# One relu per gate chunk on VectorE, weight scaling one step later, two PSUM copies on ScalarE, and a joined step in block 19 of a fused attention and gated-MLP kernel

## The chip, the cores and the metric

The kernel runs on one core of a Trainium2 chip. The core has five engines that the texts below name: TensorE (PE for matmuls, PEld for the loads of their weights), VectorE (DVE), ScalarE (ACT), GpSimd (POOL) and SyncE (SP), which issues the transfers. Each engine works through its own instruction list in order and waits on semaphores for the others. The metric is the device time of one execution in microseconds (us), and the comparison is between medians of several runs.

## The reference

A layer norm of `x` (2048 tokens, 512 features) feeds an attention over a cache (32 heads, 2048 cached keys, head size 128) and a gated MLP of width 1792 whose gate goes through a relu. Their product is added to `x`.

```python
xn = _layernorm(x)
# attention
q = (xn @ wq)                                   # 2048 x 4096, split into 32 heads
scores = einsum("bhqd,bhkd->bhqk", q, k_cache) * (128 ** -0.5)
p = softmax(scores)
s = einsum("bhqk,bhkd->bhqd", p, v_cache) @ wo
# gated MLP
gate = xn @ W_gate
up = xn @ W_up
gate = gate * (gate > 0)
g = silu((gate * up) @ W_down)
out = x + s * g
```

## The kernel before

**Attention as the main loop.** The work is cut into 128 blocks. Block `b` is one head and one quarter of the queries (512 of them), so four blocks make a head. A block has 8 pairs, numbered `p` 0 to 7; a pair is 256 keys. For a pair TensorE makes two score matmuls of 512 columns (`emit_S_tile`, L1441), ScalarE takes the exponential of both at once (L1453, 128x1024, from PSUM into `PT`), and three pairs later TensorE makes eight matmuls of 129 columns with `V_sb` (`emit_PV_tile`, L1550). `gp` counts the pairs whose scores are made, `gq = gp - 3` those whose values are. After a block VectorE divides by the row sums (L1470, L1473).

**The side work.** All the other products are set between the pairs: the query projections, the MLP's gate and up products for two of the four quarters, its down product, and the output projection. They are done in a seven-product form: a 2 by 2 product of blocks is made from seven smaller products, numbered 1 to 7, and the sums of them that VectorE adds up from PSUM. A few of the matrices' blocks are summed beforehand, on GpSimd or VectorE. So one projection is made in steps, each with one or two products:

- `emit_st(pr, c, step)` projects the queries of heads `2*pr` and `2*pr+1`, for the quarters `c` and `c+2`, in four steps (products 1 and 2; 6 and 5; 7 and 3; 4). The running sums lie in `cu` and `cv`, the results go to `QT_sb` (L871 to L928).
- `emit_gu` makes one product of one of 14 chunks of the gate and up products. In the order 1, 2, 6, 5, 7, 3, 4 it gives the gate of one quarter (`gA`, after product 2), the up of the other quarter (`uB`, product 7), its gate (`gB`, product 3) and the first quarter's up (`uA`, product 4). The relu and the product of gate and up are `gu_h` on GpSimd (L1101, L1103). Two such products share one place in the plan, so that product 1 of a chunk falls now on the first, now on the second of the two; in the second case its copy out of PSUM is on ScalarE (L1136), in the first on VectorE (L1139).
- The weights of a chunk are loaded three chunks ahead into `W2`; `gu_sums` scales them on ScalarE (L608) and sums their blocks on GpSimd (L613 to L618). It is called when `gu_later` says so: eight products after the load.
- `emit_d(Q, step)` is the down product of a quarter in four steps, with a tanh on ScalarE (L1201) and a multiplication on VectorE (L1206) one and two pairs later; `emit_hs` makes the sums it needs on VectorE (L780 to L789).
- `emit_os` is the output projection of a group of four heads, `emit_unit` a query projection of 28 smaller products for the later groups.

**What orders it.** `plan` says which items are issued at which pair `(b, p)` of the values, `side` which helpers; `qp3` is a table of places for the projection of the fourth pair of heads in the blocks 18 to 20. In the main loop the scores of pair `gp` come first, then the items, then the helpers, then the values of pair `gq`. If a block's first item has one product (`early`), the scores of the next pair are issued ahead of it.

**The ring.** The scores and the products share three PSUM slots of two banks each. A pair of scores takes one slot, released by its exponential. `emit_M` takes one slot for its list of items, released when the last of VectorE's additions out of it is done:

```python
        def emit_M(items):
            s = ring_acquire()          # waits for what released the slot last
            for fn, nb, *args in items:
                t = fn(*args, *range(k, k + nb))
                toks += t if isinstance(t, list) else [t]
            ring_tok[s] = toks
```

The slots are handed out in turn, so in a stretch with one pair and one `emit_M` at each place an `emit_M` needs the exponential of the pair before, and the next scores need the additions of the `emit_M` before.

## Time and profile before

| | |
|---|---|
| median of 3 runs | 1245.6 us (1245.51 to 1245.78) |
| profiled execution | 1245.94 us, of which its span 1244.6 us |
| PE busy in the span | 1225.7 us (98%) |
| ACT busy | 1031.3 us (83%) |
| DVE busy | 854.5 us (69%) |
| POOL busy | 715.2 us (57%) |
| granted TensorE clock | 1.00 in every stretch asked for |

A timeline row of the profile gives the start in us from the span's start, the duration in us, the engine, the source line, the operation, the tiles written and read, and how many like instructions the row merges; in square brackets stands the engine's idle time before the row, with what ended it. Matmuls are pipelined: the record of one lasts longer than the time after which the next can start, so TensorE loses time also where the records show little idle time. Lost time is read from the starts: a row's start, plus the number of its matmuls times their spacing, is when the next row could have begun.

### The profile page before, as it was taken

The numbers are of one execution on the slowest core, as the hardware profiler recorded it, in microseconds if no ns is written. First come the engines' busy times: TensorE is split into PE (matmuls) and PEld (weight loads), VectorE is DVE, ScalarE is ACT, GpSimd is POOL, SyncE is SP. The second block draws the span as 40 slices with busy tenths as digits, with TensorE's granted clock in tenths as the row PEclk, the third lists the DMA queues.
The fourth block names the chain that finished last, engine by engine and source line by source line (L and its number), as shares of the span: only waits on it lengthen the run. The fifth ranks groups of instructions, "written<-read, shape, count | busy, mean of one in ns | idle before, by whom it ended". The sixth has DMA issues, their size and how long they took to land.

```text
span 1244.6 us, 30670 instructions
## 1 busy us (share of the span) xinstructions
PE 1225.7 (98%) x12413; PEld 890.3 (72%) x12647; DVE 854.5 (69%) x1652; ACT 1031.3 (83%) x1107; POOL 715.2 (57%) x944
## 2 busy tenths in 40 slices
PE   9999999999999999999999999999999999999998
PEld 5466565776777777777777777777777777777775
DVE  6677776666666767676666667667666676666667
ACT  3457777668888988988988989989989989889994
POOL 3383999514656578547864687557862786550002
PEclk9999999999999999999999999999999999999999
DMA  9712331221322332232222332332222223444312
GB/s 275 157 31 35 73 77 31 52 43 28 56 52 52 65 69 52 48 70 51 47 38 48 77 61 48 52 70 65 53 52 49 51 53 48 52 68 74 77 36 76
DMA packets 250699, 78.14 MB, mean 63 GB/s; under 512 B 226240, under 2 KB 250560, under 8 KB 250560
## 3 DMA queue, kind: packets, MB, share of 16 engines
q1 hardware_dynamic: 249888, 75.79, 31.5%
q8 instruction: 100, 1.64, 0.6%
q10 hardware_dynamic: 672, 0.39, 0.1%
q14 instruction: 39, 0.32, 0.1%
HBM read 38.54 MB, written 2.10 MB: 33 GB/s over the span
## 4 chain that ended last, share of the span: by engine, by line
PE 85%; issue 8%; ACT 3%; POOL 2%; DVE 2%; DMA 0%; POOLq 0%; DVEq 0%
PE ps_acc L1550 33%; PE ps_r L1441 29%; PE ps_r L1322 6%; PE ps_r L1023 6%; PE ps_r L1125 3%; ACT PT L1453 3%; PE ps_r L1184 2%; PE ps_r L706 2%; PE ps_r L710 2%; PE ps_r L891 2%; PE ps_acc L809 1%; DVE UVR L1028 1%; POOL g_sb L1605 0%; POOL hT L1103 0%; POOL gB L1101 0%
## 5 line engine op out<-in xcount | busy, mean ns | idle before, releaser
L1453 ACT ACTIVATE PT<-ps_r 128x1024 bf16<-128x1024 f32 x1024 | 980.8, 1030 | 142.6 <-PE ps_r L1441 130.8
L1550 PE MATMUL ps_acc<-V_sb,PT 128*128 128x129 bf16 x8192 | 687.8, 220 | 5.3
L1550 PEld LDWEIGHTS ps_acc<-V_sb,PT 128*128 128x128 bf16 x8192 | 574.8, 98 | 144.7 <-ACT PT L1453 2.4
L1441 PE MATMUL ps_r<-QT_sb,KT_sb 128*128 128x512 bf16 x1823 | 600.6, 379 | 5.6 <-DVE QT_sb L896 0.5
L1028 DVE TENSOR_TENSOR UVR<-UVR,ps_r 128x256 f32<-128x256 f32 (+1 forms) x456 | 198.2, 454 | 160.9 <-PE ps_r L1023 156.2
L1340 DVE TENSOR_TENSOR s_acc<-s_acc,ps_r 128x512 f32<-128x512 f32 x264 | 167.7, 683 | 15.8 <-PE ps_r L1322 15.8
L1441 PEld LDWEIGHTS ps_r<-QT_sb,KT_sb 128*128 128x128 bf16 x2048 | 171.6, 98 | 8.4 <-DVE QT_sb L896 1.0
L998 POOL TENSOR_TENSOR TI<-xn_sb 128x256 f16<-128x256 f16 x96 | 66.8, 695 | 88.9 <-PE ps_r L1023 88.1
L1473 DVE TENSOR_TENSOR Onorm<-ps_acc,rz_sb 128x512 bf16<-128x512 f32 x127 | 87.8, 691 | 4.4
L1091 POOL TENSOR_TENSOR UVR<-UVR,UVR 128x1024 f32<-128x1024 f32 x12 | 28.3, 2362 | 98.8 <-DVE UVR L1028 98.8
L1028 DVE TENSOR_TENSOR QT_sb<-UVR,ps_r 128x256 bf16<-128x256 f32 x144 | 57.5, 419 | 27.8 <-PE ps_r L1023 22.8
L1605 POOL TENSOR_TENSOR g_sb<-s_acc,WX 128x512 bf16<-128x512 f32 x6 | 6.8, 1155 | 108.0 <-DVE WX L1598 108.0
L1023 PE MATMUL ps_r<-TI,SI 128*128 128x256 f16 x252 | 68.7, 273 | 0.0
L998 POOL TENSOR_TENSOR TI<-xn_sb,TI 128x256 f16<-128x256 f16 x96 | 67.8, 706 | 0.0
L998 POOL TENSOR_TENSOR TI<-xnT 128x256 f16<-128x256 bf16 x72 | 50.6, 703 | 27.2 <-PE ps_r L1023 27.2
L1470 DVE RECIPROCAL rz_sb<-ps_acc 128x4 f32<-128x4 f32 x127 | 23.2, 182 | 62.3 <-PE ps_acc L1550 59.5
L972 POOL TENSOR_SCALAR Wq_sb<-Wq_sb 128x1024 bf16<-128x1024 bf16 x12 | 33.2, 2770 | 49.8 <-DMA Wq_sb<-in_A_wq_dram 49.8
L1097 POOL TENSOR_TENSOR QT_sb<-UVR,UVR 128x512 bf16<-128x512 f32 x24 | 30.0, 1273 | 38.1 <-DVE UVR L1028 38.1
L1027 DVE COPY UVR<-ps_r 128x256 f32<-128x256 f32 x72 | 28.1, 419 | 33.6 <-PE ps_r L1023 33.6
L998 POOL TENSOR_TENSOR TI<-xnT,TI 128x256 f16<-128x256 bf16 x72 | 50.6, 703 | 0.0
L998 POOL TENSOR_TENSOR SI<-SO 128x128 f16<-128x128 f16 x96 | 49.2, 513 | 0.0
L1023 PEld LDWEIGHTS ps_r<-TI,SI 128*128 128x128 f16 x252 | 24.3, 97 | 34.1 <-DVE QT_sb L1028 6.7
(184 smaller groups left out, 1355.2 us busy)
## 6 DMA issues: line engine op xcount, KB each, us to landing
V_sb<-in_A_v_cache_dram SPq DMA_DIRECT2D x32, 512.0 KB, 4.6
Wq_sb<-in_A_wq_dram SPq DMA_DIRECT2D x16, 256.0 KB, 3.2
Wo_sb<-in_A_wo_dram SPq DMA_DIRECT2D x8, 512.0 KB, 4.6
xr_sb<-in_A_x_dram SPq DMA_DIRECT2D x16, 128.0 KB, 2.1
OT_store<-Onorm SPq DMA_TRANSPOSE x127, 2.5
Wd_sb<-in_B_W_down_dram SPq DMA_DIRECT2D x1, 1792.0 KB, 14.4
W<-in_B_W_gate_dram SPq DMA_DIRECT2D x14, 128.0 KB, 2.4
W<-in_B_W_up_dram SPq DMA_DIRECT2D x14, 128.0 KB, 3.1
```

The source lines that it names most:

```text
L972: wu_tok[(g, i)] = sem_uo.sig(pool.tensor_scalar(w, w, WSC, None, op0=ALU.mult))
L998: return sem_ui.sig(pool.tensor_tensor(dst, x, y, o))
L1023: return sem_up.sig(pe.matmul(dst, lhs, rhs, start=start, stop=stop, skip_group_check=True))
L1028: dve.tensor_tensor(dst, x, ps, ALU.add))
L1097: pool.tensor_tensor(dst, UU[:, 2 * e:2 * e + 2, :], RR[:, 2 * e:2 * e + 2, :], ALU.add))
L1125: ins = pe.matmul(ps_r[:, bank, :], L(i), R(i), start=(i == 0), stop=(i == HC - 1))
L1322: ins = pe.matmul(ps_r[:, bank, j * DH:(j + 1) * DH], L(i), R(i), start=(i == 0 and j == 0), stop=(i == GH - 1 and j == 1))
L1340: t = dve.tensor_tensor(names[k], names[k], view(bank), op)
L1441: ins = pe.matmul(ps_r[:, 2 * s + tt, :], KT_sb[h % 2][:, t * 128:(t + 1) * 128], QT_sb[qt_slot[(h, Q)]][:], start=True, stop=True)
L1453: act.activation(PT[pb][:], ps_r[:, 2 * s:2 * s + 2, :], ACTF.Exp, scale=scale / WSC)
L1473: dve.tensor_tensor(Onorm[ob][:], o_ap, rz_sb[:].to_broadcast([128, 4, Dh]), ALU.mult))
L1550: ins = pe.matmul(o_ap, PT[pb][:, tt, j * 128:(j + 1) * 128], V_sb[vb][:, t, 0:VW], start=(t == 0 and j % 2 == 0), stop=(t == KT - 1 and j ...
```

## The change

Five edits, all in the first 20 of the 128 blocks:

1. The relu of `gA` moves from GpSimd to VectorE, right behind the addition that makes `gA` (the relu of `gB` stays).
2. `gu_sums` (the scaling on ScalarE and the sums on GpSimd) is called nine products after the load, no longer eight.
3. Two copies out of PSUM move from VectorE to ScalarE: product 1 of the second half of the first projection (`cu`), and product 1 of the down product of quarter 2 (`c_u`).
4. In step 2 of every four-step projection product 3 is made before product 7, and the addition that uses it (`QT_sb` of the first head) stands ahead of the one into `cu`. In block 0 the last of the helpers `emit_hs` of quarter 2 moves from pair 4 to pair 6.
5. In the blocks 18 and 19 the projection's steps move to one or two pairs earlier; step 3 is joined with the output projection's step at the start of block 19, in one slot.

```diff
@@ emit_st @@
                 p1 = prod(1, banks[0])
                 p2 = prod(2, banks[1])
-                _wait(dve, p1)
-                st_tok["u"] = sem_qpe.sig(dve.tensor_copy(cu[:], ps_r[:, banks[0], :]))
+                if pr == 0 and c == 1:
+                    _wait_all(act, [p1, st_tok["r"]])
+                    st_tok["u"] = sem_qpa.sig(act.copy(cu[:], ps_r[:, banks[0], :]))
+                else:
+                    _wait(dve, p1)
+                    st_tok["u"] = sem_qpe.sig(dve.tensor_copy(cu[:], ps_r[:, banks[0], :]))
                 r = qt_ready[(h0, Q0)] = comb(qt_take(h0, Q0), cu[:], banks[1], waits=(p2, st_tok["u"]))
...
             if step == 2:
+                p3 = prod(3, banks[1])
                 p7 = prod(7, banks[0])
-                p3 = prod(3, banks[1])
+                qt_ready[(h0, Q1)] = comb(qt_take(h0, Q1), cv[:], banks[1], waits=(p3, st_tok["v"]))
                 st_tok["u"] = comb(cu[:], cu[:], banks[0], waits=(p7, st_tok["u"]))
-                r = qt_ready[(h1, Q1)] = comb(qt_take(h1, Q1), cv[:], banks[0], waits=(st_tok["v"],))
-                r = qt_ready[(h0, Q1)] = comb(qt_take(h0, Q1), cv[:], banks[1], waits=(p3,))
+                r = qt_ready[(h1, Q1)] = comb(qt_take(h1, Q1), cv[:], banks[0])
                 return [r]
...
-        qp3 = {18: ((2, 0), (4, 1), (6, 2)), 19: ((2, 3), (4, 4), (6, 5)), 20: ((3, 6), (5, 7))}
+        qp3 = {18: ((1, 0), (3, 1), (5, 2)), 19: ((0, 3), (2, 4), (4, 5)), 20: ((3, 6), (5, 7))}
@@ gu_h, emit_gu @@
-            _wait(pool, sem_hp.sig(pool.tensor_scalar(gate, gate, 0.0, None, op0=ALU.max)))
+            if Q == 3:
+                _wait(pool, sem_hp.sig(pool.tensor_scalar(gate, gate, 0.0, None, op0=ALU.max)))
...
                 r = gu_tok["g1"] = comb(gA[k % 2][:], u[:], waits=(gu_tok["u"], h_done.get((1, k - 2))))
+                _wait(dve, r)
+                gu_tok["gr"] = sem_gud.sig(dve.tensor_scalar(gA[k % 2][:], gA[k % 2][:], 0.0, None, op0=ALU.max))
...
-                gu_h(1, k, gA[k % 2][:], uA[k % 2][:], [r, gu_tok["g1"]])
+                gu_h(1, k, gA[k % 2][:], uA[k % 2][:], [r, gu_tok.pop("gr")])
                 if k + NW < FC:
                     gu_load(k + NW)
-                    gu_later.append((gu_pos[0] + 8, k + NW))
+                    gu_later.append((gu_pos[0] + 9, k + NW))
@@ emit_d, step 0 @@
-                _wait(dve, p1)
-                d_tok["u"] = sem_dd.sig(dve.tensor_copy(c_u[:], view(banks[0])))
+                if Q == 2:
+                    _wait(act, p1)
+                    d_tok["u"] = sem_da.sig(act.copy(c_u[:], view(banks[0])))
+                else:
+                    _wait(dve, p1)
+                    d_tok["u"] = sem_dd.sig(dve.tensor_copy(c_u[:], view(banks[0])))
@@ the plan @@
-        hs_at = {2: [(1, k, 0, 1 + k) for k in range(4)]}
+        hs_at = {2: [(1, 0, 0, 1), (1, 1, 0, 2), (1, 2, 0, 3), (1, 3, 0, 6)]}
...
                     for p, step in qp3[b]:
-                        at(b, p, (emit_st, 1 if step % 4 == 3 else 2, 3, step // 4, step % 4))
+                        q = (emit_st, 1 if step % 4 == 3 else 2, 3, step // 4, step % 4)
+                        if p:
+                            at(b, p, q)
+                        else:
+                            at(b, p, o, q)
+                            o = None
```

VectorE in block 0, from the first down addition to the block's division. `dbuf_104` is `c_u`, `dbuf_106` the first output half, `HS_sb` and `hT` the down product's sums, `cuv_86` and `cuv_87` are `cu` and `cv`. Before:

```order
L789 TENSOR_TENSOR HS_sb_58<-hT_53,HS_sb_58 128x1024
L1218 COPY dbuf_104<-ps_r 128x512
L1193 TENSOR_TENSOR dbuf_106<-dbuf_104,ps_r 128x512
L780 TENSOR_TENSOR HS_sb_58<-hT_53 128x768
L783 TENSOR_TENSOR hT_53<-hT_53 128x3x256
L896 TENSOR_TENSOR cuv_86<-cuv_86,ps_r 128x512
L896 TENSOR_TENSOR cuv_87<-cuv_86,ps_r 128x512
L786 TENSOR_TENSOR HS_sb_58<-hT_53 128x768
L1206 TENSOR_SCALAR g_sb<-dbuf_108,dbuf_106 128x2x256
L789 TENSOR_TENSOR HS_sb_58<-hT_53,HS_sb_58 128x768
L896 TENSOR_TENSOR cuv_86<-cuv_86,ps_r 128x512
L896 TENSOR_TENSOR QT_sb<-cuv_87,ps_r 128x512 x2
```

And with the change, over the same stretch:

```order
L791 TENSOR_TENSOR HS_sb_58<-hT_53,HS_sb_58 128x1024
L1203 TENSOR_TENSOR dbuf_106<-dbuf_104,ps_r 128x512
L782 TENSOR_TENSOR HS_sb_58<-hT_53 128x768
L785 TENSOR_TENSOR hT_53<-hT_53 128x3x256
L898 TENSOR_TENSOR cuv_86<-cuv_86,ps_r 128x512
L898 TENSOR_TENSOR cuv_87<-cuv_86,ps_r 128x512
L788 TENSOR_TENSOR HS_sb_58<-hT_53 128x768
L1216 TENSOR_SCALAR g_sb<-dbuf_108,dbuf_106 128x2x256
L898 TENSOR_TENSOR QT_sb<-cuv_87,ps_r 128x512
L898 TENSOR_TENSOR cuv_86<-cuv_86,ps_r 128x512
L898 TENSOR_TENSOR QT_sb<-cuv_87,ps_r 128x512
L791 TENSOR_TENSOR HS_sb_58<-hT_53,HS_sb_58 128x768
```

The copy into `c_u` has left VectorE, and the last `HS_sb` sum stands behind the three additions of the projection's step 2.

ScalarE in the gate and up stretch, where the copy of product 1 is its own (`gcu`); `W_72` is a chunk's weights, `PT` the exponentials. Before:

```order
L1453 ACTIVATE PT<-ps_r 128x1024 x6
L1136 COPY gcu_95<-ps_r 128x512
L608 ACTIVATE W_72_89<-W_72_89 128x1024
L1453 ACTIVATE PT<-ps_r 128x1024 x2
L634 ACTIVATE Wq_sb<-Wq_sb 128x1024
```

With the change:

```order
L1467 ACTIVATE PT<-ps_r 128x1024 x6
L1144 COPY gcu_95<-ps_r 128x512
L1467 ACTIVATE PT<-ps_r 128x1024
L610 ACTIVATE W_72_89<-W_72_89 128x1024
L1467 ACTIVATE PT<-ps_r 128x1024
L636 ACTIVATE Wq_sb<-Wq_sb 128x1024
```

One exponential now stands between the copy and the scaling of the weights.

TensorE at the start of block 19: `WX` with `OT_store` is the output projection's one product, `Wq_sb` with `xn_sb` the query projection's product 4. Before:

```order
L1441 MATMUL ps_r<-QT_sb,KT_sb 128x512 x4
L1322 MATMUL ps_r<-WX_119,OT_store_76 128x256 x4
L1550 MATMUL ps_acc<-V_sb,PT 128x129 x16
L1441 MATMUL ps_r<-QT_sb,KT_sb 128x512 x2
L891 MATMUL ps_r<-xn_sb,Wq_sb 128x512 x2
L1550 MATMUL ps_acc<-V_sb,PT 128x129 x8
```

With the change:

```order
L1455 MATMUL ps_r<-QT_sb,KT_sb 128x512 x2
L1336 MATMUL ps_r<-WX_119,OT_store_76 128x256 x4
L893 MATMUL ps_r<-xn_sb,Wq_sb 128x512 x2
L1564 MATMUL ps_acc<-V_sb,PT 128x129 x8
L1455 MATMUL ps_r<-QT_sb,KT_sb 128x512
```

Both products now share one slot, and the scores of the next pair are no longer issued ahead of them.

More of the change, by code (lines that the diff above doesn't have):

```diff
@@ L266, in bass_recurrent_scan__mha_block_cached__glu_gated_reglu__prompt_kernel @@
         sem_qpe = newsem()
+        sem_qpa = newsem()
+        sem_da = newsem()
         sem_rz = newsem()
@@ L927, in emit_st @@
             r = qt_ready[(h1, Q0)] = comb(qt_take(h1, Q0), cu[:], banks[0], waits=(p4, st_tok["u"]))
+            st_tok["r"] = r
             return [r]
-        qp3 = {18: ((2, 0), (4, 1), (6, 2)), 19: ((2, 3), (4, 4), (6, 5)), 20: ((3, 6), (5, 7))}
+        qp3 = {18: ((1, 0), (3, 1), (5, 2)), 19: ((0, 3), (2, 4), (4, 5)), 20: ((3, 6), (5, 7))}
         unit_order = (1, 2, 6, 5, 3, 7, 4)
```

## The prediction

> **What bounds the kernel now.** I read the page first: which engine is full?
>
> ```profile
> PE 1225.7 (98%) x12413; PEld 890.3 (72%) x12647; DVE 854.5 (69%) x1652; ACT 1031.3 (83%) x1107; POOL 715.2 (57%) x944
> ```
>
> TensorE is. The five edits lie in blocks 0 to 19, so the second view is the busy time of that stretch (columns: window, its length, then busy time and instructions of PE, PEld, DVE, ACT, POOL).
>
> ```profile
> 66.00:311.00 245.00, 241.74 (x2167) 162.40 (x2205) 172.87 (x274) 178.60 (x194) 153.35 (x139) 1.00 0.25 47
> ```
>
> TensorE is idle for 245.0 - 241.7 = 3.3 us there, and the change neither removes a matmul nor narrows one. So about 3.3 us, 0.26% of the time, is all there is to gain, and a result under 1242.3 us would contradict the profile. The third view is the timeline: where do these 3.3 us lie, and who is late there? A matmul of 512 columns starts every 0.22 us and one of 129 every 0.057 us (rows below: x4 takes 1.03 where x2 takes 0.59, and x16 takes 1.07 where x4 takes 0.39).
>
> Block 0 has the two largest gaps:
>
> ```profile
> 78.78 0.59 PE L1441 MATMUL ps_r<-QT_sb,KT_sb 128*128 128x512 bf16 x2
> 79.66 0.39 PE L891 MATMUL ps_r<-xn_sb,SW 128*128 128x512 f16 x1 [0.28 <-DVE dbuf L1193]
> ```
>
> ```profile
> 85.59 0.39 PE L1550 MATMUL ps_acc<-V_sb,PT 128*128 128x129 bf16 x4
> 86.51 0.61 PE L1441 MATMUL ps_r<-QT_sb,KT_sb 128*128 128x512 bf16 x2 [0.54 <-DVE QT_sb L896]
> ```
>
> The first could start at 78.78 + 2 x 0.216 = 79.21 and starts 0.45 late; the second at 85.59 + 4 x 0.057 = 85.82, and starts 0.69 late. Both wait for VectorE to empty a PSUM slot. Between them TensorE loses another 0.4 us in small pieces to ScalarE, which runs without a pause there:
>
> ```profile
> 73.27 2.85 ACT L1453 ACTIVATE PT<-ps_r 128x1024 bf16<-128x1024 f32 x3 [0.27 <-PE ps_r L1441]
> 79.63 0.63 ACT L1201 ACTIVATE dbuf<-dbuf 128x512 f32<-128x512 f32 x1 [3.51 <-DVE dbuf L1193]
> ```
>
> ```profile
> 82.92 3.89 ACT L1453 ACTIVATE PT<-ps_r 128x1024 bf16<-128x1024 f32 x4
> ```
>
> Its tanh waited 3.51 us for the same VectorE addition, with two exponentials queued behind it.
>
> In the gate and up stretch GpSimd's sums are late once, and ScalarE's exponential five times:
>
> ```profile
> 145.59 0.59 PE L1441 MATMUL ps_r<-QT_sb,KT_sb 128*128 128x512 bf16 x2
> 146.41 0.81 PE L1125 MATMUL ps_r<-xn_sb,SG 128*128 128x512 f16 x3 [0.22 <-POOL SG L618]
> ```
>
> ```profile
> 172.38 0.59 PE L1441 MATMUL ps_r<-QT_sb,KT_sb 128*128 128x512 bf16 x2
> 172.94 0.39 PE L1125 MATMUL ps_r<-xn_sb,SG 128*128 128x512 f16 x1
> ```
>
> ```profile
> PEld ps_r L1125 <- ACT PT L1453: 2.2, 5, 0.5
> ```
>
> The first is 146.41 - 146.02 = 0.39 us, the second 172.94 - 172.81 = 0.13 us. The waits row (total, times, longest; window 128 to 200 us) has five like the second; a load normally idles some 0.1 us between matmuls and a wait takes more than that, so I count 0.14 us for four of them and 0.20 for the fifth with its neighbour: 0.76 us. At block 19 there is one more:
>
> ```profile
> 304.42 1.03 PE L1441 MATMUL ps_r<-QT_sb,KT_sb 128*128 128x512 bf16 x4
> 305.47 0.61 PE L1322 MATMUL ps_r<-WX,OT_store 128*128 128x256 f16 x4
> 305.92 1.07 PE L1550 MATMUL ps_acc<-V_sb,PT 128*128 128x129 bf16 x16
> ```
>
> 305.47 - 305.28 = 0.19 us. The sum is 0.45 + 0.69 + 0.4 + 0.39 + 0.76 + 0.19 = 2.9 us; the rest of the 3.3 is in places that no edit touches.
>
> **The change part by part.** *Copies on ScalarE and the order in block 0.*
>
> ```profile
> 72.40 0.69 DVE L905 COPY cuv<-ps_r 128x512 f32<-128x512 f32 x1 [0.18 <-PE ps_r L891]
> 73.20 0.69 DVE L896 TENSOR_TENSOR QT_sb<-cuv,ps_r 128x512 bf16<-128x512 f32 x1
> ```
>
> ```profile
> 78.13 0.68 DVE L1218 COPY dbuf<-ps_r 128x512 f32<-128x512 f32 x1
> 78.91 0.69 DVE L1193 TENSOR_TENSOR dbuf<-dbuf,ps_r 128x512 f32<-128x512 f32 x1
> ```
>
> ```profile
> 71.97 1.02 ACT L1453 ACTIVATE PT<-ps_r 128x1024 bf16<-128x1024 f32 x1 [0.70 <-PE ps_r L1441]
> ```
>
> ```profile
> 129.50 0.58 ACT L1136 COPY gcu<-ps_r 128x512 f32<-128x512 f32 x1
> 129.96 1.07 ACT L608 ACTIVATE W<-W 128x1024 bf16<-128x1024 bf16 x1
> ```
>
> ```profile
> 73.95 0.59 PE L1441 MATMUL ps_r<-QT_sb,KT_sb 128*128 128x512 bf16 x2
> ```
>
> The first copy costs, though it leaves VectorE. On ScalarE it stands behind the exponential that ends at 72.99, takes 0.58 (as the one at 129.50 does) and ends near 73.5; VectorE had its own copy done at 73.09. The addition into `QT_sb` so ends at 74.3, not 73.89. Queued behind it are VectorE's sums `HS_sb` (+0.4), and its slot goes to the scores of the fifth pair, which TensorE starts at 73.95: +0.37 us. The second copy is free: ScalarE is idle from 76.12 to 79.63, and the product is there at 76.5. VectorE saves its 0.78 (78.13 to 78.91) but comes 0.4 later, so the down addition ends at 79.3 and not 79.60. TensorE, 0.37 late, arrives at 79.6 and no longer waits: the 0.45 is nearly all paid back at the other place. ScalarE's tanh and the exponentials behind it come 0.3 earlier, and TensorE, which follows them to 85, with them. Then step 2:
>
> ```profile
> 82.57 1.15 DVE L1206 SCALAR_TENSOR_TENSOR g_sb<-dbuf,dbuf 128x512 bf16<-128x512 f32 x1
> 83.64 1.02 DVE L789 TENSOR_TENSOR HS_sb<-hT,HS_sb 128x768 f16<-128x768 f16 x1
> 84.58 0.68 DVE L896 TENSOR_TENSOR cuv<-cuv,ps_r 128x512 f32<-128x512 f32 x1
> 85.18 1.27 DVE L896 TENSOR_TENSOR QT_sb<-cuv,ps_r 128x512 bf16<-128x512 f32 x2
> ```
>
> Without L789 ahead of them the three additions (1.95 us) end at 83.4 + 1.95 = 85.35. TensorE arrives at 85.82 - 0.3 = 85.5: the 0.69 goes, by a margin of 0.1 us. L789 then runs to 86.3 and delays the block's division, whose banks TensorE wants again only 28 matmuls later. Sum of block 0: 0.69 + 0.3 = 1.0 us (bounds: 0.5 if the margin fails and the first copy is later, 1.5 if that copy delays nobody).
>
> *Relu on VectorE.* GpSimd loses 14 instructions of 1.49 us:
>
> ```profile
> L1101 POOL TENSOR_SCALAR gA<-gA 128x512 bf16<-128x512 bf16 x14 | 20.8, 1486 | 0.0
> ```
>
> ```profile
> L436 DVE TENSOR_SCALAR xc_sb<-x_sb,mv 128x512 bf16<-128x512 bf16 x4 | 1.4, 354 | 0.1
> ```
>
> Its sums come earlier by more than the 0.39 us they were late: 0.39 gained. VectorE gains 14 instructions. The nearest row is L436, 0.354 us for the same shape with a per-partition operand; L745 below does 7 times as many elements in 1.25 us, 0.18 for this size. I take 0.25. What is queued behind it are the additions of products 6, 5 and 7, whose slots TensorE waits for. Where the relu comes late in a pair of products (7 of 14 chunks) VectorE's play is smallest:
>
> ```profile
> 173.58 0.69 DVE L1131 TENSOR_TENSOR gcv<-gcu,ps_r 128x512 f32<-128x512 f32 x1 [0.38 <-PE ps_r L1125]
> ```
>
> ```profile
> 174.98 0.68 DVE L1131 TENSOR_TENSOR uB<-gcv,ps_r 128x512 bf16<-128x512 f32 x1
> ```
>
> ```profile
> 176.04 0.59 PE L1441 MATMUL ps_r<-QT_sb,KT_sb 128*128 128x512 bf16 x2
> ```
>
> 0.38 idle before `gcv`, and 0.38 from the end of `uB` to the matmul that takes its slot, less 0.1 for the signal and 0.14 for the earlier TensorE: 0.5 us of play. 0.25 us fits. But VectorE and GpSimd hold each other up:
>
> ```profile
> 53.27 0.67 POOL L644 TENSOR_TENSOR SW<-Wq_sb 128x256 f16<-128x256 bf16 x1 [18.34 <-DVE xn_sb L589]
> 53.90 1.52 POOL L645 TENSOR_TENSOR SW<-Wq_sb 128x256 f16<-128x256 bf16 x1
> ```
>
> ```profile
> 53.64 1.25 DVE L745 TENSOR_SCALAR Wd_sb<-Wd_sb 128x3584 bf16<-128x3584 bf16 x1
> ```
>
> GpSimd's second sum takes 1.52 where the first takes 0.67: it lasts until VectorE's L745 is over, plus its own 0.67. The same kind of instruction is now added 14 times beside a busy GpSimd. Where it stands in one of the late chunks:
>
> ```profile
> 171.85 1.16 POOL L1103 TENSOR_TENSOR hT<-gB,uB 128x512 f16<-128x512 bf16 x1
> ```
>
> ```profile
> 171.69 0.69 DVE L1131 TENSOR_TENSOR gA<-gcu,ps_r 128x512 bf16<-128x512 f32 x1 [1.02 <-PE ps_r L1125]
> ```
>
> `gA` is there at 172.38, the relu wants to start at 172.5, and this product of GpSimd lasts to 173.0; with a relu less ahead of it GpSimd is about 0.2 us further, so 0.3 are waited for, and 0.3 + 0.25 is 0.05 to 0.1 more than the play. In other late chunks GpSimd is by then waiting for the scaled weights and is free. I put 0.2 us for all of them.
>
> The Trainium skill (page SBUF — State Buffer, section "Who interferes with whom") calls this an exclusive lock: a VectorE tensor_scalar in a two-port mode and a GpSimd instruction do not share, the second waits for the whole of the first. The rows of L645 agree. By that rule alone, with no look at who is where, up to a whole GpSimd instruction would be waited for, which is the second rival below.
>
> *Scaling one step later.* Where the copy is ScalarE's, copy (0.58) and scaling (1.07) stood ahead of an exponential; now the scaling stands behind it. The exponential comes 1 us earlier, so the five waits (0.76) go. The next one ends where it did, and its slot is wanted 1.75 us (four products and a pair) later: no new wait, except 0.05 us where three exponentials now go ahead. GpSimd's sums start when the scaling is done, 1.1 later, but GpSimd was the later of the two. Gain 0.7.
>
> *Block 19.*
>
> ```profile
> 304.86 0.69 DVE L1473 TENSOR_TENSOR Onorm<-ps_acc,rz_sb 128x512 bf16<-128x512 f32 x1
> ```
>
> The joined slot needs the exponential of one pair further back, so the 0.19 goes. It is released after three additions (0.64 each, as in step 2's 1.27 for two) that follow this division, which ends at 305.55: at 307.5. TensorE has the joined products (0.87) from 304.86 on, then a pair's values and scores (0.89), the next values (0.45) and scores (0.43), and wants the slot at 307.5 less 0.1 for the signal: 0.1 lost. Gain 0.1; bounds -0.2 and 0.19.
>
> The sum: 1.0 + 0.39 - 0.2 + 0.7 + 0.1 = 2.0 us. The profiled execution is 1245.94 us, 1.34 more than its span of 1244.6; the median is 0.34 less than it. 1244.6 - 2.0 + 1.34 - 0.34 = 1243.6 us.
>
> **The rivals.** *All of it comes through* (0.27). The first copy delays nobody, the relu always fits: 1.5 + 0.39 + 0.76 + 0.19 = 2.8, so 1242.8 us. For it: ScalarE's copy may start earlier than I think, 0.1 inside the exponential's end. Against it: the fifth pair's scores wait for this one slot and had nothing to spare.
>
> *The relu is held up by GpSimd each time* (0.10). In each of the 7 late chunks it waits out a relu of `gB` of 1.49 us: 1.49 + 0.25 - 0.5 = 1.2 us, 8.7 in all, so 1252.3 us. From 0.65 us a chunk (4.5 in all) the kernel is slower by more than 0.2%. Against it: after the change GpSimd is idle for part of each chunk, and in three of the seven it waits for the scaling at that time.
>
> *The waits only move* (0.20). The delayed exponentials and the later copy give back what was won, and only the 0.69 and 0.39 are kept: 1244.5 us. For it: ScalarE has the same work in the same stretch, and a copy more.
>
> **How the numbers follow.** My forecast has 0.43. About 0.2%, 2.5 us, is what a measurement tells from no change. Only the first rival (0.27) and a tenth of my own case lie below 1243.1: faster 0.30. The rest of it and the moved waits: same 0.60. Slower 0.10. The range takes in the full gain and a bad half of the relu's waits: 1242.5 to 1245.9; my own case alone has 1242.9 to 1244.4.
>
> **What would show it.** Right: the matmuls at 79.66 and 86.51 start without a wait while the fifth pair's scores start some 0.35 us later than before; no wait of L1125 for POOL's sums; the relu's row near 0.25 to 0.5 us. Wrong: a relu row over 0.8 us with waits for `uB` behind it, or new waits for `PT` one pair after each scaling.

## The result and the profile after

The kernel takes 1243.49 us (median of 19 runs, 1243.33 to 1244.19) against 1245.70 us for the kernel before (19 runs, 1245.51 to 1245.99). The ratio is 0.9983, with a 95% interval of 0.9976 to 0.9990: 2.2 us less, 0.18%. The forecast was 1243.6 us. By the bar of 0.2% that the prediction set this is the same time, to which it gave 0.60, although the interval lies wholly below 1. The profiled execution took 1243.37 us with a span of 1242.0 us, where the one before took 1245.94 us with 1244.6; the granted clock was 1.00 in both.

The first row below is the page's busy time of each engine; the second, of the windows view, is the stretch of the edits (window, length, then busy time and instructions of PE, PEld, DVE, ACT, POOL; the last three numbers are the granted clock, the share of DMA and GB/s).

```profile
PE 1224.3 (99%) x12413; PEld 890.9 (72%) x12647; DVE 858.9 (69%) x1664; ACT 1032.0 (83%) x1109; POOL 694.4 (56%) x930
```

```profile
66.00:311.00 245.00, 242.58 (x2191) 164.69 (x2228) 178.78 (x288) 180.49 (x198) 135.21 (x128) 1.00 0.26 49
```

GpSimd has lost the 14 relus (715.2 to 694.4 us). TensorE's idle time in the stretch is 245.0 - 242.6 = 2.4 us, 0.8 less than before. That cannot be the whole effect of 2.2 us, and the counts say why: beside 2228 weight loads stand only 2191 matmul records, so 37 are missing, and each gap in the records counts as idle. The measure that holds is the start times: when does a row start, and when could it have started, by the row before and its matmuls' spacing (0.216 us for 512 columns, 0.109 for 256, 0.057 for 129)? Where a matmul's record is missing, its weight load stands for it. All such late starts between 60 and 330 us, added up:

| Where TensorE starts late | before, us | after, us |
|---|---|---|
| block 0, for VectorE (79.7 and 86.6 before; 74.1 and 85.3 after) | 1.17 | 0.66 |
| block 0, for ScalarE's exponentials (81 to 85) | 0.43 | 0 |
| gate and up, for GpSimd's sums (146.4) | 0.37 | 0 |
| gate and up, for exponentials (six places) | 0.77 | 0 |
| block 19 | 0.26 | 0 |
| two places that no edit touches, and remainders | 0.39 | 0.39 |
| sum | 3.39 | 1.05 |

The sum has fallen by 2.34 us, so that the 2.2 us between the medians need no other place.

Block 0 in the timeline of the changed kernel, TensorE:

```profile
73.38 0.39 PE L1564 MATMUL ps_acc<-V_sb,PT 128*128 128x129 bf16 x4
74.07 0.59 PE L1455 MATMUL ps_r<-QT_sb,KT_sb 128*128 128x512 bf16 x2 [0.30 <-DVE QT_sb L898]
...
78.89 0.59 PE L1455 MATMUL ps_r<-QT_sb,KT_sb 128*128 128x512 bf16 x2
79.32 1.03 PE L893 MATMUL ps_r<-xn_sb,SW 128*128 128x512 f16 x4
...
84.82 0.39 PE L1564 MATMUL ps_acc<-V_sb,PT 128*128 128x129 bf16 x4
85.23 0.60 PE L1455 MATMUL ps_r<-QT_sb,KT_sb 128*128 128x512 bf16 x2
```

The fifth pair's scores could start at 73.38 + 4 x 0.057 = 73.61 and start at 74.07: a new wait of 0.45 us. The products at 79.32 start without a wait (78.89 + 0.43), where 0.45 was lost before. The scores at 85.23 are about 0.2 late; before it was 0.7.

VectorE in the same stretch:

```profile
73.23 0.69 DVE L898 TENSOR_TENSOR QT_sb<-cuv,ps_r 128x512 bf16<-128x512 f32 x1 [1.35 <-ACT cuv L908]
73.84 0.80 DVE L782 TENSOR_TENSOR HS_sb<-hT 128x1024 f16<-128x1024 f16 x1
...
77.78 0.68 DVE L1203 TENSOR_TENSOR dbuf<-dbuf,ps_r 128x512 f32<-128x512 f32 x1
78.38 1.43 DVE L782 TENSOR_TENSOR HS_sb<-hT 128x768 f16<-128x768 f16 x1
...
82.22 1.15 DVE L1216 SCALAR_TENSOR_TENSOR g_sb<-dbuf,dbuf 128x512 bf16<-128x512 f32 x1
83.30 0.68 DVE L898 TENSOR_TENSOR QT_sb<-cuv,ps_r 128x512 bf16<-128x512 f32 x1
83.90 0.67 DVE L898 TENSOR_TENSOR cuv<-cuv,ps_r 128x512 f32<-128x512 f32 x1
84.50 0.68 DVE L898 TENSOR_TENSOR QT_sb<-cuv,ps_r 128x512 bf16<-128x512 f32 x1
```

From 73.23 to 85.18 no row has idle time ahead of it: VectorE has no pause in block 0. But one row has changed that no edit touches: the sum of 768 columns at 78.38 takes 1.43 us, where it took 0.64 before. So a part of VectorE's busy time is waiting; e1 and e2 show for what.

The waits view of the weight loads in the gate and up stretch (128 to 200 us; total, times, longest) had a row of 2.2 us in 5 times for the exponentials. These are idle times of the loads, of which only a part makes a matmul late. Now it has one:

```profile
PEld ps_r L1133 <- ACT PT L1467: 0.3, 1, 0.3
```

The new relu in the view of one line (duration in ns: least, median, greatest), and one of the late chunks:

```profile
L1152 DVE TENSOR_SCALAR gA<-gA x14: 293/358/728, 104.7 to 214.3; 128x512 bf16<-128x512 bf16 x14
```

```profile
169.79 1.16 POOL L1111 TENSOR_TENSOR hT<-gB,uB 128x512 f16<-128x512 bf16 x1
...
170.47 0.62 DVE L1152 TENSOR_SCALAR gA<-gA 128x512 bf16<-128x512 bf16 x1
...
173.19 0.68 DVE L1139 TENSOR_TENSOR uB<-gcv,ps_r 128x512 bf16<-128x512 f32 x1
...
173.95 0.59 PE L1455 MATMUL ps_r<-QT_sb,KT_sb 128*128 128x512 bf16 x2
```

GpSimd's product ends at 170.95, the relu at 171.09. So it is held up as the prediction feared, 0.62 us long, and yet the scores that take the slot of `uB` are not late: the addition into `uB` ends at 173.87, 0.08 us ahead of the moment at which they can start, and that is enough.

Block 19, where step 3 now stands in one slot with the output projection:

```profile
303.06 1.29 DVE L1354 TENSOR_TENSOR s_acc<-s_acc,ps_r 128x512 f32<-128x512 f32 x2
...
304.26 0.68 DVE L898 TENSOR_TENSOR QT_sb<-cuv,ps_r 128x512 bf16<-128x512 f32 x1
...
304.63 0.59 PE L1455 MATMUL ps_r<-QT_sb,KT_sb 128*128 128x512 bf16 x2
...
305.06 1.03 PE L893 MATMUL ps_r<-xnT,Wq_sb 128*128 128x512 bf16 x4
```

The three additions end at 304.94, and the next user of the slot starts at 305.06 = 304.63 + 0.43, on time.

### The profile page after: what moved, and what is told of

Its sections match the earlier page's. It is cut to its first block, busy times and chain, and to the rows that moved or that the text cites. A ratio compares the mean times of both kernels' runs of the same rounds, so it can differ in the third digit from the quotient of the medians.

```text
span 1242.0 us, 30671 instructions
## 1 busy us (share of the span) xinstructions
PE 1224.3 (99%) x12413; PEld 890.9 (72%) x12647; DVE 858.9 (69%) x1664; ACT 1032.0 (83%) x1109; POOL 694.4 (56%) x930
## 4 chain that ended last, share of the span: by engine, by line
PE 87%; issue 8%; ACT 3%; DVE 1%; POOL 1%; POOLq 0%; DVEq 0%
PE ps_acc L1564 33%; PE ps_r L1455 29%; PE ps_r L1336 6%; PE ps_r L1030 6%; PE ps_r L1133 3%; ACT PT L1467 3%; PE ps_r L1194 3%; PE ps_r L708 2%; PE ps_r L712 2%; PE ps_r L893 2%; PE ps_acc L811 1%; DVE UVR L1035 1%; POOL g_sb L1619 1%; PE ps_r L459 0%; PE ps_r L525 0%
## 5 line engine op out<-in xcount | busy, mean ns | idle before, releaser
L1484 DVE RECIPROCAL rz_sb<-ps_acc 128x4 f32<-128x4 f32 x127 | 23.2, 183 | 61.7 <-PE ps_acc L1564 59.0
```

## Experiments

Seven runs undo one part of the change, one doubles a cost, one makes one edit alone, three go on from what was found. "Lost" is the sum of late starts from 60 to 330 us in the profiled execution, as in the table above (3.39 before, 1.05 after). The medians of the kernel before lay between 1245.68 and 1245.79 us over the sets of runs, so a tenth of a microsecond between medians says nothing. The changed kernel was timed in one set of runs, the others in four later sets, and the intervals of the ratios reach some 1.1 us to either side: they do not tell e1 to e7 and e9 to e11 from the changed kernel. What tells them apart is where, and by how much, TensorE starts late in the one profiled execution of each.

| Run | median, us | ratio to before (95%) | against the changed kernel, us | lost, us |
|---|---|---|---|---|
| e1 first copy on VectorE | 1243.55 | 0.9982 (0.9973 to 0.9991) | +0.06 | 1.04 |
| e2 second copy on VectorE | 1243.78 | 0.9985 (0.9977 to 0.9994) | +0.29 | 1.27 |
| e3 old order in step 2 | 1243.48 | 0.9982 (0.9974 to 0.9991) | -0.01 | 1.04 |
| e4 helper at pair 4 | 1244.46 | 0.9990 (0.9981 to 0.9999) | +0.97 | 2.12 |
| e5 relu on GpSimd | 1244.43 | 0.9990 (0.9981 to 0.9998) | +0.94 | 1.56 |
| e6 scaling one product earlier | 1244.28 | 0.9989 (0.9980 to 0.9998) | +0.79 | 2.24 |
| e7 old places in blocks 18 and 19 | 1243.82 | 0.9985 (0.9976 to 0.9993) | +0.33 | 1.32 |
| e8 relu twice | 1251.05 | 1.0042 (1.0028 to 1.0056) | +7.56 | 8.19 |
| e9 multiplication later | 1243.40 | 0.9982 (0.9973 to 0.9992) | -0.09 | 0.85 |
| e10 e1 and e9 | 1243.18 | 0.9979 (0.9970 to 0.9988) | -0.31 | 0.75 |
| e11 e10 and two helpers later | 1242.89 | 0.9978 (0.9969 to 0.9987) | -0.60 | 0.47 |
| e12 before, with the relu's move alone | 1245.62 | 0.9999 (0.9990 to 1.0008) | | 3.00 |

**e1: the first copy back on VectorE.**

```diff
-                if pr == 0 and c == 1:
-                    _wait_all(act, [p1, st_tok["r"]])
-                    st_tok["u"] = sem_qpa.sig(act.copy(cu[:], ps_r[:, banks[0], :]))
-                else:
-                    _wait(dve, p1)
-                    st_tok["u"] = sem_qpe.sig(dve.tensor_copy(cu[:], ps_r[:, banks[0], :]))
+                _wait(dve, p1)
+                st_tok["u"] = sem_qpe.sig(dve.tensor_copy(cu[:], ps_r[:, banks[0], :]))
```

> The changed kernel with the first copy (`cu`, second half of the first projection) back on VectorE. In the changed kernel the fifth pair's scores start at 74.09 and lose 0.45 us, and VectorE then works without a pause until its addition ends at 85.18, for which TensorE waits 0.21. Theory (the copy is on the wrong engine, since it stands behind an exponential): VectorE's own copy is done some 0.37 earlier, the 0.45 goes, VectorE's whole chain is 0.37 earlier, and the later wait is 0.21 + 0.45 - 0.37 = 0.29. Net gain 0.37 us: 1243.1 us. Rival (VectorE is full until 85.2, so the wait only moves to the end of its chain): the 0.45 turns up again at 85, where 0.66 are lost: 1243.5 us, no change.

The time is the same: the rival is right about the time, though not about the place. The 0.45 at 74 goes, but 0.35 are lost at 82.2 and 0.29 at 85.5. TensorE at the first of these (81.36 + 0.43 = 81.79), then VectorE and GpSimd:

```profile
81.36 0.59 PE L1451 MATMUL ps_r<-QT_sb,KT_sb 128*128 128x512 bf16 x2
82.12 0.60 PE L893 MATMUL ps_r<-xnT,SW 128*128 128x512 bf16 x2 [0.17 <-DVE cuv L898]
```

```profile
73.12 0.69 DVE L898 TENSOR_TENSOR QT_sb<-cuv,ps_r 128x512 bf16<-128x512 f32 x1
73.73 1.17 DVE L782 TENSOR_TENSOR HS_sb<-hT 128x1024 f16<-128x1024 f16 x1
```

```profile
73.69 0.67 POOL L620 TENSOR_TENSOR SG<-W,SG 128x256 f16<-128x256 bf16 x1
```

This execution runs 0.27 us later than the profiled one of the changed kernel from its start-up on (`hT` at 71.47, there 71.20), so the addition comes 0.38 us earlier than there (73.12 against 73.23 + 0.27). The helper behind it then lasts 1.17 us in place of 0.80 and eats that up. It ends 0.54 us after GpSimd's sum (74.36), as in the changed kernel (73.42 + 0.67 = 74.09, the helper's end 74.64). GpSimd, not the copy, decides when VectorE's chain goes on.

**e2: the second copy back on VectorE.**

```diff
-                if Q == 2:
-                    _wait(act, p1)
-                    d_tok["u"] = sem_da.sig(act.copy(c_u[:], view(banks[0])))
-                else:
-                    _wait(dve, p1)
-                    d_tok["u"] = sem_dd.sig(dve.tensor_copy(c_u[:], view(banks[0])))
+                _wait(dve, p1)
+                d_tok["u"] = sem_dd.sig(dve.tensor_copy(c_u[:], view(banks[0])))
```

> The changed kernel with the second copy (`c_u` of the down product of quarter 2) back on VectorE. Theory (VectorE's chain in block 0 has no pause from 73.2 to 85.2, so that what is put into it comes out at its end): 0.6 to 0.7 us more for the addition that releases the slot at 85.18; the loss there grows from 0.21 to about 0.85, and the tanh comes 0.65 later: 1244.1 us. Rival (the products at 79.32 have a margin of 0.88 us over the down addition, so the copy is covered wherever it is done): 1243.5 us, no change.

Both were wrong, and the reason is the same neighbour. Here are VectorE's rows and GpSimd's scaling of weights:

```profile
78.45 2.77 POOL L638 TENSOR_SCALAR Wq_sb<-Wq_sb 128x1024 bf16<-128x1024 bf16 x1
...
78.65 0.69 DVE L1203 TENSOR_TENSOR dbuf<-dbuf,ps_r 128x512 f32<-128x512 f32 x1
...
79.26 0.64 DVE L782 TENSOR_TENSOR HS_sb<-hT 128x768 f16<-128x768 f16 x1
79.37 0.63 ACT L1211 ACTIVATE dbuf<-dbuf 128x512 f32<-128x512 f32 x1 [3.39 <-DVE dbuf L1203]
```

The sum of 768 columns ends at 79.90, 1.45 us after the start of GpSimd's scaling. In the changed kernel the scaling starts at 78.36 and the sum, begun 0.02 later, ends at 79.81: again 1.45.

```profile
78.36 2.77 POOL L638 TENSOR_SCALAR Wq_sb<-Wq_sb 128x1024 bf16<-128x1024 bf16 x1
```

Whatever VectorE does in between is free, so its 0.78 us for the copy do not lengthen its chain. What remains is the tanh: it comes 0.88 us later than in the changed kernel (78.49; 0.09 of this is the later start of this execution), the exponentials behind it make TensorE late in four places between 81.0 and 84.7 (0.26 + 0.09 + 0.05 + 0.03 = 0.43 us), and TensorE no longer waits at 85. The net is 0.22 us, 0.29 by the medians. The copy is worth that, and by way of ScalarE's tanh.

**e3 and e4: the order of step 2, and the place of the helper.**

```diff
 e3
-                p3 = prod(3, banks[1])
                 p7 = prod(7, banks[0])
-                qt_ready[(h0, Q1)] = comb(qt_take(h0, Q1), cv[:], banks[1], waits=(p3, st_tok["v"]))
+                p3 = prod(3, banks[1])
                 st_tok["u"] = comb(cu[:], cu[:], banks[0], waits=(p7, st_tok["u"]))
-                r = qt_ready[(h1, Q1)] = comb(qt_take(h1, Q1), cv[:], banks[0])
+                r = qt_ready[(h1, Q1)] = comb(qt_take(h1, Q1), cv[:], banks[0], waits=(st_tok["v"],))
+                r = qt_ready[(h0, Q1)] = comb(qt_take(h0, Q1), cv[:], banks[1], waits=(p3,))
 e4
-        hs_at = {2: [(1, 0, 0, 1), (1, 1, 0, 2), (1, 2, 0, 3), (1, 3, 0, 6)]}
+        hs_at = {2: [(1, 0, 0, 1), (1, 1, 0, 2), (1, 2, 0, 3), (1, 3, 0, 4)]}
```

> The changed kernel with step 2 of the projection in its old order (product 7 ahead of product 3, and the addition of product 3 last); the helper stays at pair 6. Theory (the 0.69 us at 86.5 went because the helper went behind the three additions; their order is neutral, since VectorE has no pause and the slot is released after all three): 1243.5 us, and 0.2 lost at 85.3 as now. Rival (the order itself brought it): the loss at 85.3 rises by some 0.5 us: 1244.0 us.

> The changed kernel with the last of the helpers `emit_hs` of quarter 2 back at pair 4 of block 0, ahead of step 2's additions; their new order stays. Theory: 0.53 to 0.95 us more ahead of the addition that ends at 85.18, so 0.75 to 1.15 us lost at 85.3 in place of 0.21: 1244.0 to 1244.4 us. Rival (the order of the products does the work, the helper's place does not matter): 1243.5 us.

The theory holds in both. The order is neutral (0.20 us lost at 85.3, as now). The helper's place is the largest single part of the change; with it at pair 4, ahead of the additions, the scores wait:

```profile
83.60 1.02 DVE L791 TENSOR_TENSOR HS_sb<-hT,HS_sb 128x768 f16<-128x768 f16 x1
...
86.47 0.60 PE L1455 MATMUL ps_r<-QT_sb,KT_sb 128*128 128x512 bf16 x2 [0.86 <-DVE QT_sb L898]
```

By the starts they lose 1.05 us there, 0.84 more than in the changed kernel. Another 0.2 us of this run's lost time stands at 61.7, which no edit touches.

**e5: the relu of `gA` back on GpSimd.**

```diff
-                _wait(dve, r)
-                gu_tok["gr"] = sem_gud.sig(dve.tensor_scalar(gA[k % 2][:], gA[k % 2][:], 0.0, None, op0=ALU.max))
...
-            if Q == 3:
-                _wait(pool, sem_hp.sig(pool.tensor_scalar(gate, gate, 0.0, None, op0=ALU.max)))
+            _wait(pool, sem_hp.sig(pool.tensor_scalar(gate, gate, 0.0, None, op0=ALU.max)))
...
-                gu_h(1, k, gA[k % 2][:], uA[k % 2][:], [r, gu_tok.pop("gr")])
+                gu_h(1, k, gA[k % 2][:], uA[k % 2][:], [r, gu_tok["g1"]])
```

> The changed kernel with the relu of `gA` back on GpSimd, the scaling still nine products after the load. Theory (the relu's move is worth what GpSimd's sums were late): before, one load of SG waited, 0.37 us in all, and the sums now start some 1.1 us later than before because of the scaling, so the same one comes back and the next closest (0.64 us of margin before) gets close: 0.4 to 0.9 us lost in the gate and up stretch, where the changed kernel loses nothing; 1243.9 to 1244.4 us. Rival (the later scaling alone took that wait away, or the relu costs VectorE as much as it saves GpSimd): 1243.5 us.

The one wait for the sums is back and has grown from 0.37 to 0.48 us:

```profile
145.30 1.02 PE L1132 MATMUL ps_r<-xn_sb,SG 128*128 128x512 f16 x4 [0.33 <-POOL SG L620]
```

The median is a little beyond the expected range. In its profile two more waits stand far behind the edits, 0.22 us at 722 and 0.21 at 1131, in code that is the same in both kernels; the changed kernel has none there.

**e6 and e7: the scaling, and the blocks 18 and 19.**

```diff
 e6
-                    gu_later.append((gu_pos[0] + 9, k + NW))
+                    gu_later.append((gu_pos[0] + 8, k + NW))
 e7
-        qp3 = {18: ((1, 0), (3, 1), (5, 2)), 19: ((0, 3), (2, 4), (4, 5)), 20: ((3, 6), (5, 7))}
+        qp3 = {18: ((2, 0), (4, 1), (6, 2)), 19: ((2, 3), (4, 4), (6, 5)), 20: ((3, 6), (5, 7))}
```

> The changed kernel with the weights' scaling eight products after the load again. Theory: where ScalarE also makes the copy, copy and scaling stand ahead of an exponential again, and the five or six waits of 0.08 to 0.15 us of the kernel before are back: 0.6 to 0.8 us more, 1244.2 us. Rival (those waits went because the relu shifted the chunks' work, not because of the scaling's place): 1243.5 us.

> The changed kernel with the old table of places for the fourth projection in blocks 18 and 19, step 3 not joined. Theory: the wait at the start of block 19 is back, 0.20 us at the output projection's product and 0.05 behind it: 1243.75 us, and 0.25 us more lost time at 303. Rival (it was won by the shifted arrival of TensorE, not by the join): no lost time there, 1243.5 us.

Both as the theory has it. With the earlier scaling the same six exponentials are late as before (0.15 + 0.14 + 0.14 + 0.12 + 0.08 + 0.14 = 0.77 us; the other lost time in its profile, 0.3 more at each of 62 and 241, lies in places that no edit touches, and the 0.2 at 85 is not there). The waits view (126 to 200 us) has the row of the kernel before back:

```profile
PEld ps_r L1133 <- ACT PT L1467: 2.2, 5, 0.5
```

With the old places in block 19, 0.19 us are lost again at 303.2 (302.12 + 0.86 = 302.98) and 0.06 at 305.0:

```profile
302.12 1.03 PE L1455 MATMUL ps_r<-QT_sb,KT_sb 128*128 128x512 bf16 x4
303.18 0.61 PE L1336 MATMUL ps_r<-WX,OT_store 128*128 128x256 f16 x4
```

**e8: the relu made twice.**

```diff
-                gu_tok["gr"] = sem_gud.sig(dve.tensor_scalar(gA[k % 2][:], gA[k % 2][:], 0.0, None, op0=ALU.max))
+                gr = sem_gud.sig(dve.tensor_scalar(gA[k % 2][:], gA[k % 2][:], 0.0, None, op0=ALU.max))
+                _wait(dve, gr)
+                gu_tok["gr"] = sem_gud.sig(dve.tensor_scalar(gA[k % 2][:], gA[k % 2][:], 0.0, None, op0=ALU.max))
```

> The changed kernel with the relu of `gA` made twice on VectorE, one behind the other (the second changes nothing in the values). In the changed kernel a free relu takes 0.29 us, and 8 of the 14 lie beside a GpSimd product: those end 0.15 us after that product does, up to 0.73 us long; the three tightest slots keep only 0.10 to 0.16 us for the scores that take them, which is just enough. Theory (VectorE's relu waits out the whole GpSimd instruction that is running): in the 7 late chunks the second relu meets GpSimd's next product, of 1.2 us, and is 1.0 to 1.3 us long; with 0 to 0.5 us of play 0.6 to 1.2 us are lost in each, 4 to 8 us in all: 1247.5 to 1251.5 us. Rival (a relu costs its own 0.29 us or less, and the wait for GpSimd is had once only): some 0.25 us in the three tightest chunks and nothing elsewhere, 1244.2 us.

The theory holds, near its upper end. The second relu by the view of one line, and one chunk on VectorE and GpSimd:

```profile
L1154 DVE TENSOR_SCALAR gA<-gA x14: 293/1125/1129, 105.3 to 222.0; 128x512 bf16<-128x512 bf16 x14
```

```profile
174.84 1.21 POOL L1111 TENSOR_TENSOR hT<-gA,uA 128x512 f16<-128x512 bf16 x1
```

```profile
174.40 0.63 DVE L1152 TENSOR_SCALAR gA<-gA 128x512 bf16<-128x512 bf16 x1
175.07 1.13 DVE L1154 TENSOR_SCALAR gA<-gA 128x512 bf16<-128x512 bf16 x1
```

GpSimd's product ends at 176.05, the second relu at 176.20. In 8 of the 14 chunks it is 1.13 us long and ends 0.15 us after the product. The lost time rises by 8.19 - 1.05 = 7.1 us; another 0.3 us stands at 890, behind the edits. The first relu had just fitted: a second one, which by its own work costs 0.29 us, makes the kernel 0.4% slower than before.

**e9, e10, e11: taking VectorE's chain in block 0 apart.** The first `g_sb` multiplication of quarter 2 (1.15 us, with nothing near that waits for it) goes behind step 2's additions; then the first copy goes back to VectorE as well; then two helpers go one pair later.

```diff
 e9, e10, e11
-                defer(2, mult)
+                defer(5 if Q == 2 and r == 0 and c == 0 else 2, mult)
 e10, e11: and the edit of e1
 e11
-        hs_at = {2: [(1, 0, 0, 1), (1, 1, 0, 2), (1, 2, 0, 3), (1, 3, 0, 6)]}
+        hs_at = {2: [(1, 0, 0, 1), (1, 1, 0, 3), (1, 2, 0, 4), (1, 3, 0, 6)]}
```

> The changed kernel with one more VectorE instruction moved: the first multiplication `g_sb` of quarter 2 (1.15 us at 82.22, ahead of step 2's additions) comes three pairs later, at pair 6 behind them. Theory (VectorE has no pause from 73.2 to 85.2, and what stands ahead of the last addition sets the slot): the addition ends about 1 us earlier, the 0.21 at 85.3 goes, the 0.45 at 74.1 stays: 1243.3 us. Rival (VectorE is held by GpSimd and by the products' arrival, so the gap just opens elsewhere): 1243.5 us, or more if the block's division comes too late.

> The changed kernel with the multiplication three pairs later, as in the run before, and the first copy back on VectorE. With that copy on VectorE alone, 0.45 was saved at 74 and 0.35 + 0.29 lost at 82.2 and 85.5 in place of 0.21. Theory: the 0.35 at 82.2 stays, since the multiplication stands behind it, the loss at 85.5 goes: 0.30 us less than the changed kernel, 1243.2 us. Rival (the later place of TensorE takes it back at block 1's start): 1243.5 us.

> As the run before, and two of the helpers `emit_hs` (0.56 and 0.59 us) one pair later, at pairs 3 and 4, so that the first of them stands behind step 1's additions. Theory: these end 0.5 us earlier, the 0.35 at 82.2 goes too, and block 0 loses nothing: 0.66 us less than the changed kernel, 1242.85 us. Rival (in their new places the helpers run beside GpSimd's sums and wait them out, 0.4 to 0.7 us each): 0.2 to 0.7 us are lost at 85 again, 1243.0 to 1243.5 us.

In the profiles all three do what the theory says: the loss at 85.3 goes (e9 keeps 0.45 at 74.3, e10 keeps 0.35 at 82.1), and in e11 only 0.08 us of block 0 are left, in two waits for exponentials. The medians follow: 1243.40 (0.1 more than expected), 1243.18 and 1242.89. Where the first copy's return alone brought nothing, it brings 0.2 by the medians once the multiplication is out of the way, though only 0.10 by the late starts (0.85 to 0.75). The helpers' move brings 0.3 more. The version of e11 beats both kernels, the changed one by 0.6 us. TensorE in it:

```profile
81.20 0.59 PE L1451 MATMUL ps_r<-QT_sb,KT_sb 128*128 128x512 bf16 x2
81.63 0.59 PE L893 MATMUL ps_r<-xnT,SW 128*128 128x512 bf16 x2
...
84.56 0.39 PE L1560 MATMUL ps_acc<-V_sb,PT 128*128 128x129 bf16 x4
84.78 0.59 PE L1451 MATMUL ps_r<-QT_sb,KT_sb 128*128 128x512 bf16 x2
85.21 1.69 PE L1190 MATMUL ps_r<-WdT,HS_sb 128*128 128x256 f16 x14
```

The products at 81.63 and the scores at 84.78 start on time (81.20 + 0.43; 84.56 + 0.23), and block 1's down product comes at 85.21, in the changed kernel at 85.67.

**e12: the relu's move alone, in the kernel before.** The edit is that of e5 in the other direction.

> The kernel before with the first edit alone: the relu of `gA` on VectorE, all else as it was. Undoing this edit in the changed kernel cost 0.94 us of the median, of which 0.48 were one wait for GpSimd's sums in the gate and up stretch and 0.43 two waits at 722 and 1131, where both kernels run the same code. Theory: alone it is worth the one wait that it takes away, 0.37 us, and the exponential waits stay: 1245.3 us against 1245.7. Rival A (the late waits belong to GpSimd's relu): they would show in the kernel before too, which has none there, so A needs a gain above 0.37: 1244.9 us. Rival B (beside the earlier scaling VectorE's relu costs something): 1245.5 us or more.

The theory is right in place and not in sum. The wait at 146 is gone, the relu costs nothing, and the lost time up to 330 us falls by 3.39 - 3.00 = 0.39 us. But the median is only 0.17 us below that of the kernel before, timed together with it (1245.79), since at 774.8 a wait of 0.20 us stands that was not there:

```profile
774.37 1.27 DVE L1028 TENSOR_TENSOR QT_sb<-UVR,ps_r 128x256 bf16<-128x256 f32 x3 [0.81 <-PE ps_r L1023]
...
774.84 0.10 PEld L1023 LDWEIGHTS ps_r<-TI,SO 128*128 128x128 f16 x1 [0.53 <-DVE QT_sb L1028]
```

It is of the same kind as the two late ones of e5: a projection unit's weights wait for additions that VectorE started late. Rival A falls with it, since these waits appear with the relu on either engine. What moves them wasn't tried.

## Why the prediction was right, and where it was not

**What there was to gain.** The list of waits was right: 2.9 us by the prediction's rows, 3.0 by all starts. The bound of 3.3 us was right by chance only: it came from busy time, in which 38 missing records (2167 matmuls beside 2205 loads) count as idle, while a wait that lies under the record of the matmul before does not.

**Block 0, forecast 1.0 us, measured 0.94.** The sum came out right by luck, for two of its terms are off in opposite directions. The 0.69 was to go with 0.1 to spare; 0.2 of it stayed. The step that failed is the end of the three additions at 83.4 + 1.95 = 85.35, set against TensorE's arrival at 85.5. The profiled execution of the changed kernel runs 0.34 us earlier from its start-up on (`hT` at 71.20, before at 71.54). In the times of the kernel before, its additions ended at 85.18 + 0.34 = 85.52, so 0.17 later than forecast, and TensorE could have gone on at 85.05 + 0.34 = 85.39, so 0.1 earlier. The prediction had VectorE 0.3 us earlier, since the second copy had left it. It gained nothing there, because of the sum of 768 columns. This sum ends at 79.81 + 0.34 = 80.15 in the changed kernel and at 80.16 before, in both 1.45 us after the start of GpSimd's scaling. Before:

```profile
78.71 2.77 POOL L636 TENSOR_SCALAR Wq_sb<-Wq_sb 128x1024 bf16<-128x1024 bf16 x1
79.52 0.64 DVE L780 TENSOR_TENSOR HS_sb<-hT 128x768 f16<-128x768 f16 x1
```

TensorE came earlier than thought because ScalarE's small waits went wholly, 0.43 us and not 0.3; this is what made up for the 0.2 in the sum.

The first copy's price was 0.45 (forecast 0.37). What I called its second effect, VectorE 0.4 us later behind it, did not exist: e1 shows the helper waiting for GpSimd in either case. So the copy that was costed at 0.37 and was to pay for itself at 79 is worth nothing by itself, and the gain of this block is the helper's new place (0.84 in e4) and the second copy (0.22 in e2). That copy was called free, and is; its gain through the tanh was foreseen.

**The product order**, which stands in the fourth edit, is worth nothing with the helper in its new place (e3). The prediction had put the 0.69 on L789 going behind the additions, which is what e4 confirms.

**Relu, forecast 0.39 - 0.2, measured 0.37 - 0.** GpSimd's late sums were sized right. The relu's price is 0.29 us where it is free, 0.62 in the chunk that the prediction worked through (it said 0.3 of waiting and 0.25 of work). The wrong term is the 0.2 us lost for it: the play of 0.5 us was enough. In the three tightest chunks the addition ends 0.07 to 0.13 us ahead of the moment at which the scores can start, and they start on time (the 0.10 to 0.16 in the expectation of e8 is 0.03 more than the records give). That it was close is shown by e8: the second rival's mechanism is real, and one more relu in each chunk brings it, with 7.1 us. One row was read wrongly for it: GpSimd's L645 ended at 55.42, 0.53 us after VectorE's L745 (54.89), and not its whole 0.67 after it.

The Trainium skill (page SBUF — State Buffer, section "Who interferes with whom") has VectorE and GpSimd share a port pair under a lock held for a whole instruction. The rows agree for GpSimd's instructions on two tensors: every relu of the changed kernel that met one ended 0.15 us after it. They do not for its instructions on one tensor, where VectorE goes on before the end (last section).

**Scaling, forecast 0.7, measured 0.77** (e6: 0.79 of the median). No new wait came, not even the 0.05 that was set aside.

**Block 19, forecast 0.1, measured 0.26.** The places were right to a few hundredths. The three additions took 1.84 us from the division's end and not 1.95, so the slot is free when TensorE wants it, and the 0.1 to be lost there was not.

**The rivals.** "All of it comes through" was nearest in gate, up and block 19, and wrong about the first copy. "The waits only move" is right for that copy alone. The medians of the parts do not add up: undoing them one at a time costs 0.06 + 0.29 + 0 + 0.97 + 0.94 + 0.79 + 0.33 = 3.4 us, more than the 2.2 that they bring together. By the late starts at the places of the edits they nearly do: 0 + 0.22 + 0 + 0.84 + 0.48 + 0.77 + 0.25 = 2.6 us against 2.3, of which 0.1 is that the later scaling makes GpSimd's relu dearer (0.48 in e5, 0.37 before). The rest of the 3.4 is the 0.43 of late waits in e5 and some 0.1 between medians and late starts in most runs; what causes these is open.

**The signs.** Of those that the prediction named, the products at 79.66 start without a wait, no load waits for GpSimd's sums, no new wait for `PT` follows a scaling, and the fifth pair's scores are late, by 0.45. The scores at 86.51 are still 0.2 late, and single relus take up to 0.73 us, more than the 0.25 to 0.5 and less than the 0.8 that would have meant wrong.

## What to carry to other kernels

Where an engine has no pause over a stretch, moving one instruction off it can leave its later results where they were (both copies here, ahead of sums that GpSimd held up). Ask which later instruction sets its pace, and move what stands ahead of the last result that someone waits for. Before an instruction goes to VectorE, look at what GpSimd runs at that time: beside an instruction with two input tensors the relu's price was the time to that one's end, not its own. Gains of a few tenths of a microsecond are read from start times at their place, since later waits come and go by as much.

## What the runs showed of the hardware

- A VectorE relu (128x512, 16 bit) took 0.29 us when GpSimd was idle. Beside a GpSimd instruction on two input tensors (seven products and a sum) it ended 0.15 us after that one, in 8 of the 14 chunks of the changed kernel, and beside a product again in 8 with the second relu of e8. VectorE's sum of 1024 columns ended 0.55 us after GpSimd's sum in the kernels before and after and in e1.
- GpSimd's scaling of 128x1024 (2.77 us) let VectorE's sum go on before its end: it ended 1.45 us after the scaling's start in the changed kernel (begun at 0.02) and in e2 (begun at 0.81).
- A matmul that waited started 0.05 to 0.06 us after the end of the instruction that it waited for (in the kernel before, the exponential that ends at 172.89 and the product at 172.94, the addition that ends at 86.45 and the scores at 86.51). An end 0.07 us ahead of the moment at which the matmul could start was early enough: nothing was lost in the three tightest chunks of the changed kernel, which had 0.07, 0.08 and 0.13. In the kernel before 0.08 us were lost where the exponential ended 0.015 us behind that moment (190.61).
